# Packed attention and a GELU feed-forward on one core: pair 0's output tiles stored by four transfers of 32 rows each, its values loaded in two transfers, and a new order of all engines

## The chip, the cores and the metric

The kernel runs on one core of one Trainium2 chip. The metric is the device time of one launch in microseconds (us); a time given for a kernel is the median of several runs. A core has five engines with a program each: TensorE (PE, with its weight loads PEld), VectorE (DVE), ScalarE (ACT), GpSimd (POOL) and SyncE (SP). In this kernel all transfers are issued from SP's queue, and sixteen DMA engines move the bytes.

## What is computed

```python
def sm_attn(qq, kk, vv):
    s = scale * np.matmul(qq, kk.transpose(0, 1, 3, 2))
    s = s - np.max(s, axis=-1, keepdims=True)
    a = np.exp(s)
    a = a / (np.sum(a, axis=-1, keepdims=True) + 1e-09)
    return np.matmul(a, vv)
p_packed = sm_attn(p, k, v)            # 32 packed queries over 576 keys
out = sm_attn(q, p_packed, p_packed)   # 576 queries over the 32 packed rows

x = out.transpose(0, 2, 1, 3).reshape(4608, 512)
h = x @ w_in                           # w_in 512 x 2048
g = 0.5 * h * (1.0 + erf(h / sqrt(2)))
return g @ w_out                       # w_out 2048 x 512
```

q, k and v are 8 batches x 8 heads x 576 x 64, p is 8 x 8 x 32 x 64, all fp32. The output is 4608 x 512.

## The kernel before

The eight batches are worked off in four pairs (`pr` 0 to 3). A pair has 1152 tokens, which make nine output tiles of 128 x 512, kept in the accumulators `acc_<pr>_<i>`. d_ff is worked off in four units of 512 columns in each pair, so there are 16 units of 8 steps, 32 steps a pair. A unit makes h from the attention weights `a2T` and from `wp` (the packed rows times w_in, made from `wps`), h in six or twelve products of 128 x 288 (L1080); ACT and DVE make g of it; and the products with w_out (`o`, L1133 to L1135, three for each tile since fp32 values are split in a high and a low part) go to PSUM and are added to the accumulators by DVE (L1197). Tile 4 of a pair, the edge tile, gets half its rows from each batch; it is made last in a unit (`o_edge`).

The attention of the next pair is worked in between the products of the present one: p is loaded (L501) and transposed on PE (`pTm`, L507), k and q are loaded (L424 for pair 0, one transfer each; L434 for the later pairs, four transfers of 32 partitions each) and transposed (on PE in pair 0, by DVE later), v is loaded (`load_values`). The weights of a unit come as raw words in pair 0 (`wraw`, L939 and L943), are decoded into a high and a low part, and stored to scratch memory (`ws<-w`, L995); from pair 1 on they are reloaded from there (`w<-ws`, L917).

For pair 0, rows are held in another order than in memory: a tile has four blocks of 32 rows, each of which goes to every 18th row of the output. `finish.store` (L1204 to L1209) writes such a tile in one transfer of 4 x 32 x 512, and tile 4, whose blocks lie in two batches, in two of 2 x 32 x 512. The later pairs write 128 x 512 in one transfer (L1204). The values of pair 0 are loaded by `sixths` (L484): 96 partitions, four heads, 384 numbers in a row (1536 bytes).

The order of the instructions on each engine is set at build time by a planner, `Order`. Every piece of work is an `Op` with an engine, a model cost and a due step; the tables `FIRST` (pair 0), `SECOND` (pair 1) and `LATER` (pairs 2 and 3) hold the due steps of the attention's parts, and `LEAD`, `PATIENCE`, `STEADY`, `DMA_SLACK` and `DMA_EARLY` are rules for all of them. The planner keeps the model that eight DMAs at most are under way (`DMA_DEPTH`): in the program, each transfer on SP is issued when the one eight places ahead of it has landed. Where the model finds PE without work before the first g is used, `keep_warm` puts in products on constants (`idle<-still`, L1053), which I call fillers; in the start, other products are also made twice, once into a tile named `idle`.

Of the kernel before, what the change touches and what calls it, by code (L numbers as in the profile page):

```python
# [19 lines left out]
P = 128  # L20
B, H, S, D = 8, 8, 576, 64
PK = 32
# [3 lines left out]
NB32 = S // 32  # L26
# [13 lines left out]
PE, ACT, DVE, POOL, DMA = "PE", "ACT", "DVE", "POOL", "DMA"  # L40
# [2 lines left out]
DMA_FIRST, DMA_ISSUE, DMA_START, DMA_END, DMA_RATE = 2.0, 0.5, 0.6, 0.9, 390e3  # L43

DMA_DEPTH = 8
DMA_SLACK, DMA_EARLY = 4.0, 60.0
TABLE_SWITCH = 1.3
PE_START, PE_WINDOW, PE_LEAST = 1.0, 3.41, {True: 0.45, False: 0.9}
IDLE, IDLE_END = 0.11, 150.0
# [2 lines left out]


LATER = {
    "p": (-39.26, -15.86),
    "k": (5.65, 1.31, 12.01, 17.16),
    "v": (-16.69, 1.61, 22.03, 27.81),
    "q": (22.44, 3.57, 12.78, 22.93),
    "scores1": (14.09, -17.44),
    "softmax1": (-9.54, 26.63, -24.19, 26.51),  # L60
    "packed": (-23.89, -22.94, 27.45, 26.53),
    "scores2": (-14.65, 21.78),
    "softmax2": (-24.19, -0.03, 50.16, 22.74),
    "weights2": (29.03, 29.95, 1.17, -15.25),
    "groups1": ((0,), (1,), (2,), (3,)),
    "groups2": ((0, 1), (2, 3)),
}

SECOND = {
    "p": (-3.61, -10.72),  # L70
    "k": (3.41, 0.25, 20.0, -56.69),
    "v": (-22.26, 3.59, 18.15, 21.3),
    "q": (23.11, 21.3, 21.6, 7.77),
    "scores1": (-9.82, -56.39),
    "softmax1": (-18.51, 6.58, 9.15, -41.24),
    "packed": (-34.85, 15.81, -9.92, 9.75),
    "scores2": (9.45, 41.41),
    "softmax2": (-24.65, -40.94, -56.99, -10.3),
    "weights2": (22.04, 35.39, 45.19, 24.77),
    "groups1": ((0, 1), (2, 3)),  # L80
    "groups2": ((0, 1), (2, 3)),
}

AHEAD = 12
LEAD = {"load": 18.5, "decode": -13.4, "packed_w_in": 60.1}

PATIENCE = {PE: -23.4, ACT: -9.6, DVE: 24.2, POOL: 77.7, DMA: 2.3}
STEADY = {PE: 45.5, ACT: -6.9, DVE: -15.7, POOL: 21.7, DMA: -10.7}

FIRST = {  # L90
    "p": (-210.0, -176.51),
    "k": (-233.78, -212.77, -176.19, -173.89),
    "v": (-186.03, -193.47, -169.61, -153.18),
    "q": (-191.58, -185.11, -162.68, -170.97),
    "w": (-199.98, -187.11, -191.97, -183.54, -185.21, -163.81, -39.7, -122.51),
    "scores1": (-152.97, -209.53, -175.46, -197.7),
    "softmax1": (-160.37, -231.56, -191.55, -215.45),
    "packed": (-171.95, -190.55, -210.03, -179.55),
    "scores2": (-212.47, -194.44, -189.26, -176.97),
    "softmax2": (-173.59, -208.41, -192.11, -160.67),  # L100
    "weights2": (-189.27, -209.73, -175.76, -227.21),
    "decode": (-202.23, -169.16, -49.02, -171.27, -8.54, -68.27, -164.29, -169.26),
    "packed_w_in": (-177.55, -176.04, -176.11, -179.23),
    "weights_split": (-184.5, -170.67, -166.39, -169.56),
    "groups1": ((0,), (1,), (2,), (3,)),
    "groups2": ((0,), (1,), (2,), (3,)),
    "gpsimd": (0, 1),
    "copy": ("DVE", "DVE", "DVE", "ACT"),
    "banks": (False, False, True, False),
    "turn": {"k": ("ACT", "DVE", "ACT", "ACT"), "q": ("ACT", "DVE", "ACT", "ACT")},  # L110
}

# [51 lines left out]
class Order:  # L164
# [4 lines left out]
    def __init__(self):  # L169
# [4 lines left out]
        self.warm, self.window, self.busy, self.idle = False, PE_WINDOW, 0.0, None  # L174
        self.port, self.tiled, self.patience = 0.0, False, PATIENCE
        self.free[PE] = PE_START
# [5 lines left out]
    def start(self, task, then=None):  # L182
        self.open += 1
        self.advance(task, then, None, None)

    def fire(self, event):
        event.count -= 1
        if event.count == 0:
            for fn in event.waiting:
                self.at(self.now, fn)  # L190
# [121 lines left out]
def packed_attention_gelu_ffn(ctx: ExitStack, tc: tile.TileContext, q, k, v, p, w_in, w_out, out):  # L312
# [12 lines left out]
    nc = tc.nc  # L325
# [142 lines left out]
    def values_of(t):  # L468

        main = t[:, 0:16 * D].rearrange("p (g t d) -> p g t d", g=4, t=4)  # L470
        tail = t[:64, 16 * D:20 * D].rearrange("p (g d) -> p g d", g=4)
        return main, tail

    def sixths_of(t):

        if len(t.shape) > 2:
            t = t.rearrange("p a b c -> p (a b c)").bitcast(F32)
        return t[:96, 0:24 * D].rearrange("p (g t d) -> p g t d", g=4, t=6)

    def load_values(s, step):  # L480
        heads = slice(4 * s.hh, 4 * s.hh + 4)

        def sixths(t):
            nc.sync.dma_start(  # L484
                sixths_of(t).rearrange("p g t d -> p g (t d)"), v[s.b, heads].rearrange("g (p t) d -> p g (t d)", t=6))

        def fn(t):
            main, tail = values_of(t)
            nc.sync.dma_start(
                main.rearrange("p g t d -> p g (t d)"), v[s.b, heads, 0:512].rearrange("g (p t) d -> p g (t d)", t=4))  # L490
            nc.sync.dma_start(tail, v[s.b, heads, 512:S].rearrange("g p d -> p g d"))

        cost, fn = ((1, 640e3), sixths) if s.b < 2 else ((2, 900e3, 0.6), fn)
        s.v = yield Op(DMA, cost, step, fn, [(s.v_ring, f"v_{s.n}")])
        fire(s.v_loaded)

# [317 lines left out]
    def held(task, step):  # L814
        if step >= 1:
            yield reached[min(int(step), NU * 8 - 1)]
        yield from task

    def attention(pr, plan):
# [11 lines left out]
        for s in ss:  # L831
            s.mx, s.mx2 = mx, mx2
            s.v_ring = wps[1] if (s.b, s.hh) == (0, 1) else vraws
            start(held(load_values(s, plan["v"][s.i]), plan["v"][s.i]))
# [64 lines left out]
    def parts_of(i):  # L899

        return 2 if i < 2 else 1
# [6 lines left out]
    def weight(u, i, load_steps, steps):  # L908


        ring_, home, k = (wis, wi, i) if i < 2 else (wos, wo, i - 2)
        n, f = f"{u}_{i}", u % NF
        if u >= NF:
            yield stored[f, i]
            home[u, k] = yield Op(
                DMA, (1, 524e3), steps[0],
                lambda t: nc.sync.dma_start(t.bitcast(F32), scratch[f, i]), [(ring_, f"w_{n}")])  # L917
            for part in range(parts_of(i)):
                fire(w_ready[u, i, part])
            return  # L920
        yield [decode(u, i, part, *at) for part, at in enumerate(zip(load_steps, steps))]
        d = scratch[f, i] = dram.tile([P, 2, FB], F32, name=f"ws_{f}_{i}")
        start(keep(f, i, d, home[u, k], steps[-1] + 4))
# [213 lines left out]
    def output_steps():  # L1137
        for n in range(NU * 8):
# [3 lines left out]
            if n == STEPS + NC4:  # L1142
                order.patience = STEADY
            if n % STEPS == 0:
# [44 lines left out]
    def finish(u, i, t, ring_, n):  # L1189
        pr, f = divmod(u, NF)  # L1190
        x = t[:, 0] if ring_ is wide else t
        if f == 0:
            acc[pr, i] = yield Op(ACT, 0.48, n, lambda a: nc.scalar.copy(a, x), [(accs, f"acc_{pr}_{i}")])
            ring_.give(t)
            return
        a = acc[pr, i]
        yield Op(DVE, 0.6, n, lambda: nc.vector.tensor_tensor(a, x, a, ALU.add))  # L1197
        ring_.give(t)
        if f == NF - 1:
            r0 = pr * 2 * S + i * P  # L1200

            def store():
                if pr > 0:
                    nc.sync.dma_start(out[r0:r0 + P], a)  # L1204
                    return
                for r, m in ((0, P),) if i != 4 else ((0, 64), (64, 64)):
                    b, n0 = divmod((r0 + r) // PK, NB32)
                    rows = out[b * S:(b + 1) * S].rearrange("(x n) d -> n x d", n=NB32)[n0:n0 + m // PK]
                    nc.sync.dma_start(rows, a[r:r + m])  # L1209

            yield Op(DMA, (1, 262e3), n, store)
            accs.give(a)


# [16 lines left out]
    for u in range(NU):  # L1231
        for i in range(6):
            use = 8 * u + (2 * i - 6 if i < 2 else i - 3)
            if u == 0:
                part = slice(2 * i, 2 * i + 2) if i < 2 else slice(2 + i, 3 + i)
                start(weight(u, i, FIRST["w"][part], FIRST["decode"][part]))
            else:
                start(held(weight(
                    u, i, *([use + k - LEAD[name] for k in range(parts_of(i))] for name in ("load", "decode"))),
                    8 * u - AHEAD))  # L1240
# [6 lines left out]
        else:  # L1247
            for j in range(2):
                start(held(packed_w_in(u, j, 0, 8 * u + 4 * j - LEAD["packed_w_in"]), 8 * u + 4 * j - AHEAD))
    start(hidden_steps())  # L1250
# [34 lines left out]
```

## Time and profile before

| | |
|---|---|
| median of 3 runs | 750.29 us (749.0, 750.29, 750.57) |
| the profiled execution's own time | 751.05 us |
| its span, from the first to the last instruction | 749.3 us |
| mean granted clock of PE | 0.991 of full speed |
| transfers | 106.77 MB, 142 GB/s over the span |

The profile comes from one execution. PE, DVE, ACT, POOL and SP are the engines named above; L12 is a line of the kernel. A row of a timeline or of the chain has the start in us, the length in us, and what ran; in brackets is the idle time ahead of it and what ended it. "SPq" is time in which SP's queue issues transfers. A row of a table of stretches has the stretch, its length, busy us and number of instructions of PE, PEld, DVE, ACT and POOL, then the granted clock of PE, the busy share of the sixteen DMA engines and GB/s. In a table of one tile, three numbers between slashes are the shortest, the median and the longest duration in ns, and then stand the first and last start in us. Rows of transfers end with how long it took from issue to landing.

### The profile page before, as it was taken

The numbers are of one execution on the slowest core, as the hardware profiler recorded it, in microseconds if no ns is written. First come the engines' busy times: TensorE is split into PE (matmuls) and PEld (weight loads), VectorE is DVE, ScalarE is ACT, GpSimd is POOL, SyncE is SP. The second block draws the span as 40 slices with busy tenths as digits, with TensorE's granted clock in tenths as the row PEclk, the third lists the DMA queues.
The fourth block names the chain that finished last, engine by engine and source line by source line (L and its number), as shares of the span: only waits on it lengthen the run. The fifth ranks groups of instructions, "written<-read, shape, count | busy, mean of one in ns | idle before, by whom it ended". The sixth has DMA issues, their size and how long they took to land.

```text
span 749.3 us, 13343 instructions
## 1 busy us (share of the span) xinstructions
PE 730.7 (98%) x5369; PEld 592.8 (79%) x5369; DVE 399.1 (53%) x608; ACT 363.2 (48%) x606; POOL 153.0 (20%) x330
## 2 busy tenths in 40 slices
PE   8899999999999699999999999999999999999998
PEld 6667788787877578887877888877877888888886
DVE  3689958777778231435484622454474821333332
ACT  4577785657654433355453543364543543333221
POOL 1353545455410101101100111100011110111010
PEclk9899999999999999999999999999999999999999
DMA  9977966489924577189223986179233603122022
GB/s 272 329 264 137 238 144 225 169 232 243 210 101 150 147 111 173 31 188 140 77 96 115 239 116 165 34 178 165 45 113 117 238 3 101 68 71 72 1 91 92
DMA packets 154449, 106.77 MB, mean 142 GB/s; under 512 B 122644, under 2 KB 130324, under 8 KB 154388
## 3 DMA queue, kind: packets, MB, share of 16 engines
q1 hardware_dynamic: 154388, 105.93, 55.0%
q8 instruction: 42, 0.69, 0.4%
q14 instruction: 19, 0.16, 0.1%
HBM read 83.89 MB, written 22.02 MB: 141 GB/s over the span
## 4 chain that ended last, share of the span: by engine, by line
PE 92%; DMA 4%; SPq 3%; DVE 1%; ACT 1%; issue 0%; ACTq 0%
PE h L1080 25%; PE o L1133 17%; PE o L1135 15%; PE o L1134 15%; PE wps L1014 4%; DMA p<-in_p_dram 2%; PE s L535 2%; SPq L434 2%; PE o_edge L1133 2%; PE o_edge L1135 2%; PE o_edge L1134 2%; DMA v<-in_v_dram 2%; PE idle L1053 2%; PE pp L677 1%; PE e1Tm L636 1%; PE h L1071 1%
## 5 line engine op out<-in xcount | busy, mean ns | idle before, releaser
L1080 PEld LDWEIGHTS h<-a2T,wp 128*128 128x128 f32 x1488 | 209.8, 188 | 9.6
L1080 PE MATMUL h<-a2T,wp 128*128 128x288 f32 x1488 | 216.5, 295 | 0.0
L1103 ACT ACTIVATE graw<-h 128x576 f32<-128x576 f32 x127 | 82.8, 652 | 273.4 <-PE h L1080 216.7
L1133 PE MATMUL o<-w,g 128*128 128x512 f32 x508 | 207.2, 408 | 0.0
L1135 PE MATMUL o<-w,g 128*128 128x512 f32 x508 | 199.7, 393 | 0.0
L1134 PE MATMUL o<-w,g 128*128 128x512 f32 x508 | 199.4, 393 | 0.0
L1112 DVE TENSOR_TENSOR g<-graw,g 128x512 fp32r<-128x512 f32 x128 | 90.4, 706 | 200.2 <-ACT g L1110 193.6
L1123 POOL CAST t<-graw 128x64 fp32r<-128x64 f32 x128 | 36.2, 282 | 493.9 <-ACT graw L1103 399.6
L1133 PEld LDWEIGHTS o<-w,g 128*128 128x128 f32 x508 | 95.7, 188 | 42.4 <-issue 24.7
L1135 PEld LDWEIGHTS o<-w,g 128*128 128x128 f32 x508 | 95.6, 188 | 22.6 <-DVE g L1112 0.9
L1134 PEld LDWEIGHTS o<-w,g 128*128 128x128 f32 x508 | 95.9, 189 | 15.0
L1197 DVE TENSOR_TENSOR acc<-o,acc 128x512 f32<-128x512 f32 x96 | 63.9, 686 | 40.2 <-PE o L1135 39.9
L1110 ACT CAST g<-graw 128x512 fp32r<-128x512 f32 x128 | 79.4, 621 | 3.8 <-PE o L1135 0.9
L1030 DVE TENSOR_TENSOR wp<-wps,wp 128x1024 fp32r<-128x1024 f32 (+1 forms) x32 | 37.8, 1187 | 20.9 <-ACT wp L1025 20.8
L1124 POOL TENSOR_TENSOR t<-graw,t 128x64 fp32r<-128x64 f32 x128 | 45.6, 356 | 10.2
L1025 ACT CAST wp<-wps 128x1024 fp32r<-128x1024 f32 (+1 forms) x31 | 30.8, 1000 | 16.6 <-PE wps L1014 16.6
L1014 PE MATMUL wps<-w,pp 64*32 64x512 f32 (+1 forms) x544 | 34.9, 576 | 0.0
L976 POOL TENSOR_TENSOR w<-wt 128x512 int32<-128x512 int32 x16 | 22.5, 1404 | 42.3 <-DVE wt L962 38.4
L1053 PE MATMUL idle<-still 128*128 128x256 bf16 x205 | 29.3, 293 | 1.1 <-DVE still L394 1.1
L949 ACT ACTIVATE wt<-wraw 128x512 f32<-128x512 f32 x32 | 21.7, 679 | 15.3 <-DMA wraw<-in_moe_w_in_dram 9.1
L957 DVE TENSOR_SCALAR wt<-wt 128x512 int32<-128x512 int32 x32 | 28.3, 883 | 1.1
L984 POOL TENSOR_TENSOR wt<-wt 128x512 int32<-128x512 int32 x16 | 21.8, 1361 | 28.5 <-DVE wt L962 25.6
(126 smaller groups left out, 673.1 us busy)
## 6 DMA issues: line engine op xcount, KB each, us to landing
w<-ws SPq DMA_DIRECT2D x72, 512.0 KB, 5.2
ws<-w SPq DMA_DIRECT2D x24, 512.0 KB, 5.9
out_dram<-acc SPq DMA_DIRECT2D x35, 256.0 KB, 2.1
wraw<-in_moe_w_in_dram SPq DMA_DIRECT2D x16, 512.0 KB, 9.1
wraw<-in_moe_w_out_dram SPq DMA_DIRECT2D x16, 512.0 KB, 4.2
k<-in_k_dram SPq DMA_DIRECT2D x48, 144.0 KB, 5.8
q<-in_q_dram SPq DMA_DIRECT2D x48, 144.0 KB, 4.6
v<-in_v_dram SPq DMA_DIRECT2D x12, 512.0 KB, 4.7
```

The costliest lines, as they stand in the source:

```text
L1014: nc.tensor.matmul(t[r0:r0 + 32, hh, :m], lhsT=pp[b][rows, hh, r0:r0 + 32], rhs=wi[u, hh][rows, g, cols], start=True, stop=True)
L1030: yield Op(DVE, 0.16 + 1.04 * m / FB, step, lambda: nc.vector.tensor_tensor(lo, x, hi.bitcast(F32), ALU.subtract))
L1053: nc.tensor.matmul(bank(t)[:, :256], lhsT=still[:, :P], rhs=still, start=True, stop=True)
L1080: nc.tensor.matmul(t[:, half, :HALF], lhsT=w[:, wpart, ch, fc], rhs=a2T[b, ch][:, apart, half * HALF:(half + 1) * HALF], start=ch == 0 and ...
L1103: lambda raw: nc.scalar.activation(raw.rearrange("p (a n) -> p a n", a=2), t[:, :, :HALF], AF.Gelu),
L1110: g = yield Op(ACT, 0.52, lead, lambda g: nc.scalar.copy(g[:, 0], main), [(gts, f"g_{n}")])
L1112: DVE, 0.6, lead, lambda: nc.vector.tensor_tensor(g[:, 1], main, g[:, 0].bitcast(F32), ALU.subtract),
L1124: nc.gpsimd.tensor_tensor(dst[:, 1], side, dst[:, 0].bitcast(F32), ALU.subtract)
L1133: nc.tensor.matmul(t, lhsT=g[0], rhs=w[:, 0], start=first, stop=False)
L1134: nc.tensor.matmul(t, lhsT=g[0], rhs=w[:, 1], start=False, stop=False)
L1135: nc.tensor.matmul(t, lhsT=g[1], rhs=w[:, 0], start=False, stop=last)
L1197: yield Op(DVE, 0.6, n, lambda: nc.vector.tensor_tensor(a, x, a, ALU.add))
```

## The change

The nine output tiles of pair 0 are each stored by four transfers of one 32-row block, so that ten transfers become 36, and their cost in the planner's model is changed with it. The values of pair 0 are loaded in two transfers, the first four and the last two of each six rows (runs of 1024 and of 512 bytes). All due steps of the three tables and the rules `LEAD`, `PATIENCE` and `STEADY` have other numbers, `DMA_SLACK` and `DMA_EARLY` are smaller, and in pair 0 other engines make some copies. Lines from L484 on stand three lines lower in the new kernel.

```diff
-DMA_SLACK, DMA_EARLY = 4.0, 60.0
+DMA_SLACK, DMA_EARLY = 2.0, 50.0
...
-LEAD = {"load": 18.5, "decode": -13.4, "packed_w_in": 60.1}
+LEAD = {"load": 41.5, "decode": -5.8, "packed_w_in": 12.3}
...
-    "v": (-186.03, -193.47, -169.61, -153.18),
+    "v": (-249.99, -74.38, -178.71, -155.31),
...
-    "gpsimd": (0, 1),
-    "copy": ("DVE", "DVE", "DVE", "ACT"),
-    "banks": (False, False, True, False),
+    "gpsimd": (0,),
+    "copy": ("ACT", "DVE", "DVE", "DVE"),
+    "banks": (False, True, True, True),
...
         def sixths(t):
-            nc.sync.dma_start(
-                sixths_of(t).rearrange("p g t d -> p g (t d)"), v[s.b, heads].rearrange("g (p t) d -> p g (t d)", t=6))
+            src = v[s.b, heads].rearrange("g (p t) d -> p g t d", t=6)
+            for part in (slice(0, 4), slice(4, 6)):
+                nc.sync.dma_start(
+                    sixths_of(t)[:, :, part].rearrange("p g t d -> p g (t d)"),
+                    src[:, :, part].rearrange("p g t d -> p g (t d)"))
...
-        cost, fn = ((1, 640e3), sixths) if s.b < 2 else ((2, 900e3, 0.6), fn)
+        cost, fn = ((2, 700e3), sixths) if s.b < 2 else ((2, 900e3, 0.6), fn)
...
-                for r, m in ((0, P),) if i != 4 else ((0, 64), (64, 64)):
+                for r in range(0, P, PK):
                     b, n0 = divmod((r0 + r) // PK, NB32)
-                    rows = out[b * S:(b + 1) * S].rearrange("(x n) d -> n x d", n=NB32)[n0:n0 + m // PK]
-                    nc.sync.dma_start(rows, a[r:r + m])
-
-            yield Op(DMA, (1, 262e3), n, store)
+                    rows = out[b * S:(b + 1) * S].rearrange("(x n) d -> n x d", n=NB32)[n0]
+                    nc.sync.dma_start(rows, a[r:r + PK])
+
+            yield Op(DMA, (1, 262e3) if pr else (4, 262e3), n, store)
```

SP's queue at the end of pair 0, before the change: `acc` are the output tiles, `w` and `ws` the reloaded weights, `k` and `p` those of the batches that come next; "x4" is four transfers.

```order
L917 DMA w_4_2887<-ws_4_845 128x1024
L1209 DMA out_dram<-acc_8_1414 4x32x512
L917 DMA w_5_2896<-ws_5_834 128x1024
L917 DMA w_2_2902<-ws_2_1260 128x1024
L917 DMA w_3_2905<-ws_3_1340 128x1024
L1209 DMA out_dram<-acc_4_1454 2x32x512 x2
L434 DMA k_1_2941<-in_k_dram 32x36x32 x4
L501 DMA p_2979<-in_p_dram 128x2x64 x2
```

The same place in the new order:

```order
L434 DMA k_0_2912<-in_k_dram 32x36x32 x4
L1212 DMA out_dram<-acc_7_1348 32x512 x4
L1212 DMA out_dram<-acc_8_1375 32x512 x4
L1212 DMA out_dram<-acc_4_1418 32x512 x4
L920 DMA w_4_3028<-ws_4_923 128x1024
L920 DMA w_5_3040<-ws_5_938 128x1024
L920 DMA w_2_3052<-ws_2_1297 128x1024
L920 DMA w_3_3054<-ws_3_1347 128x1024
L504 DMA p_3167<-in_p_dram 128x2x64 x2
```

The k load has moved ahead of the stores and the four reloads of w behind all of them, so that p, the last row, follows the reloads of w instead of k.

PE around the transpose of that p (`pTm`), before:

```order
L1135 MATMUL o_3_2922<-w_5_2896,g_3008 128x512
L1080 MATMUL h_3074<-a2T_0_2996,wp_1_2760 128x288 x6
L1080 MATMUL h_3074<-a2T_1_2947,wp_1_2760 128x288 x6
L507 MATMUL pTm_3093<-ident,p_2979 128x128 x2
L1133 MATMUL o_0_3098<-w_2_2516,g_3061 128x512
```

PE there in the new order:

```order
L1138 MATMUL o_2_3203<-w_2_2367,g_3093 128x512
L1136 MATMUL o_3_3208<-w_2_2367,g_3093 128x512
L1137 MATMUL o_3_3208<-w_2_2367,g_3093 128x512
L1138 MATMUL o_3_3208<-w_2_2367,g_3093 128x512
L510 MATMUL pTm_3212<-ident,p_3167 128x128 x2
L1136 MATMUL o_0_3176<-w_3_2371,g_3127 128x512
```

Counted from unit 3's edge tile, 18.8 us of PE's work stood ahead of the transpose; now it is 20 groups of three `o` products, six sets of twelve `h` and two of `wps`.

SP's queue in the start, before (`v_1` are the values of batch 0's heads 4 to 7, `p_151` is the second batch's p):

```order
L424 DMA k_0_85<-in_k_dram 128x1152
L424 DMA k_1_87<-in_k_dram 128x1152
L501 DMA p_91<-in_p_dram 128x2x64 x2
L943 DMA wraw_0_0_98<-in_moe_w_in_dram 128x2x512
L484 DMA v_1_102<-in_v_dram 96x4x384
L943 DMA wraw_1_0_107<-in_moe_w_in_dram 128x2x512
L424 DMA q_0_111<-in_q_dram 128x1152
L943 DMA wraw_0_1_115<-in_moe_w_in_dram 128x2x512
L484 DMA v_0_121<-in_v_dram 96x4x384
L939 DMA wraw_2_0_136<-in_moe_w_out_dram 128x1024
L943 DMA wraw_1_1_139<-in_moe_w_in_dram 128x2x512
L501 DMA p_151<-in_p_dram 128x2x64 x2
```

The new order from the second batch's p on (`p_144`; ahead of it stand the same kinds of loads with one v, `v_0`, in two pieces):

```order
L504 DMA p_144<-in_p_dram 128x2x64 x2
L424 DMA q_1_171<-in_q_dram 128x1152
L424 DMA k_0_198<-in_k_dram 128x1152
L942 DMA wraw_2_0_218<-in_moe_w_out_dram 128x1024
L942 DMA wraw_3_0_236<-in_moe_w_out_dram 128x1024
L424 DMA k_1_257<-in_k_dram 128x1152
L486 DMA v_1_275<-in_v_dram 96x4x256
L486 DMA v_1_275<-in_v_dram 96x4x128
```

`v_1` has moved from the fifth row of SP's order to its eighteenth and nineteenth. On PE, the fillers of the start are 231 where they were 205, and the required products are the same.

More of the change, by code (lines that the diff above doesn't have):

```diff
@@ L54 @@
 LATER = {
[L55 to L65, printed above, removed]
+    "p": (11.96, 4.31),
+    "k": (9.37, 6.72, -0.79, 5.76),
+    "v": (4.46, 5.97, 10.35, 23.09),
+    "q": (7.94, 14.96, 23.74, 28.45),
+    "scores1": (-2.56, 15.38),
+    "softmax1": (8.43, -1.96, 4.16, 5.99),
+    "packed": (-50.68, -7.0, 15.26, 19.97),
+    "scores2": (22.79, 15.93),
+    "softmax2": (-77.33, -62.89, 23.22, 15.85),
+    "weights2": (32.15, -50.98, -6.98, 38.51),
+    "groups1": ((0, 1, 2, 3),),
     "groups2": ((0, 1), (2, 3)),
@@ L69 @@
 SECOND = {
[L70 to L81, printed above, removed]
+    "p": (20.75, 3.34),
+    "k": (7.37, -42.06, 10.92, 22.21),
@@ L82 @@
+    "v": (8.64, 9.54, 12.08, 14.62),
+    "q": (24.0, -36.23, 19.77, 24.5),
+    "scores1": (-7.96, 8.69),
+    "softmax1": (23.58, 28.48, 10.35, 11.22),
+    "packed": (13.43, 9.46, -19.64, 17.8),
+    "scores2": (-42.32, 23.44),
+    "softmax2": (3.08, -54.42, 7.07, 36.08),
+    "weights2": (7.31, 23.91, -34.4, 27.85),
+    "groups1": ((0,), (1,), (2,), (3,)),
+    "groups2": ((0,), (1,), (2,), (3,)),
 }
 AHEAD = 12
-LEAD = {"load": 18.5, "decode": -13.4, "packed_w_in": 60.1}
-PATIENCE = {PE: -23.4, ACT: -9.6, DVE: 24.2, POOL: 77.7, DMA: 2.3}
@@ L88 @@
-STEADY = {PE: 45.5, ACT: -6.9, DVE: -15.7, POOL: 21.7, DMA: -10.7}
+LEAD = {"load": 41.5, "decode": -5.8, "packed_w_in": 12.3}
+PATIENCE = {PE: -50.7, ACT: -58.2, DVE: 28.6, POOL: 30.2, DMA: -16.5}
+STEADY = {PE: 50.0, ACT: -44.9, DVE: 8.1, POOL: -12.5, DMA: 13.9}
 FIRST = {
-    "p": (-210.0, -176.51),
-    "k": (-233.78, -212.77, -176.19, -173.89),
-    "v": (-186.03, -193.47, -169.61, -153.18),
[L94 to L105, printed above, removed]
+    "p": (-317.54, -182.89),
+    "k": (-327.51, -303.62, -196.02, -185.2),
+    "v": (-249.99, -74.38, -178.71, -155.31),
+    "q": (-216.51, -212.03, -93.83, -161.52),
+    "w": (-194.95, -219.42, -192.91, -163.65, -152.43, -145.84, -71.43, -169.98),
+    "scores1": (-221.37, -193.05, -72.18, -73.16),
+    "softmax1": (-51.37, 6.81, -347.66, -175.1),
+    "packed": (-180.43, -262.75, -182.09, 5.22),
+    "scores2": (-233.03, -212.25, -155.17, -251.0),
+    "softmax2": (-146.14, -327.21, -189.22, -190.15),
+    "weights2": (-183.99, -138.74, -180.16, -74.68),
+    "decode": (-178.03, -74.98, -180.05, -168.82, -193.1, -214.82, -193.35, 17.95),
+    "packed_w_in": (-192.13, -218.39, -190.45, -146.14),
+    "weights_split": (-94.13, -184.63, -65.79, -335.34),
+    "groups1": ((0, 1), (2, 3)),
```

## The prediction

> **What bounds the kernel now.** I read the page's busy shares, slices and chain of work first, then the waits of PE, then the chain around the longest wait.
>
> ```profile
> PE 730.7 (98%) x5369; PEld 592.8 (79%) x5369; DVE 399.1 (53%) x608; ACT 363.2 (48%) x606; POOL 153.0 (20%) x330
> PE   8899999999999699999999999999999999999998
> PEclk9899999999999999999999999999999999999999
> PE 92%; DMA 4%; SPq 3%; DVE 1%; ACT 1%; issue 0%; ACTq 0%
> ```
>
> PE is busy 98% of a span of 749.3 us and is 92% of the chain; no other engine is above 53%. So the time is PE's own work plus the little time in which it waits or runs at a lower clock. Only two places show in the slices: the first two or three, and slice 14 with its "6". The waits of PE over the whole run name them (what waited for what, us in total, times, the longest):
>
> ```profile
> PE pTm L507 <- DMA p<-in_p_dram: 10.6, 3, 6.6
> PE e1Tm L636 <- ACT graw L1103: 1.4, 2, 0.7
> PE idle L677 <- DMA v<-in_v_dram: 0.9, 1, 0.9
> ```
>
> The timeline of PE shows where the two long waits for p end, and a table of stretches shows the clock around them (busy us per engine with counts, then granted clock, DMA share, GB/s):
>
> ```profile
> 24.01 0.66 PE L507 MATMUL pTm<-ident,p 128*128 128x128 f32 x2 [3.38 <-DMA p<-in_p_dram]
> 262.79 0.66 PE L507 MATMUL pTm<-ident,p 128*128 128x128 f32 x2 [6.60 <-DMA p<-in_p_dram]
> ```
>
> ```profile
> 23.20:30.00 6.80, 5.99 (x28) 5.30 (x29) 2.61 (x6) 4.83 (x10) 1.35 (x2) 0.50 1.01 404
> 258.70:265.50 6.80, 2.71 (x8) 2.26 (x9) 2.40 (x3) 0.00 (x0) 0.00 (x0) 0.50 1.29 163
> 62.00:237.00 175.00, 175.00 (x1274) 140.50 (x1273) 138.34 (x198) 110.89 (x188) 72.45 (x103) 1.00 0.73 184
> 0.00:62.00 62.00, 55.02 (x687) 41.61 (x688) 39.44 (x78) 36.83 (x77) 24.15 (x31) 0.94 0.91 279
> ```
>
> Each wait has a half-clock stretch with it. The second costs 6.60 us of idleness and, of the 2.71 us that PE then ran at 0.50, half: 1.35 us. From 62 to 237 us PE waits for nothing at full clock. The first 62 us are a start in which the transfers are the limit (DMA share 0.91).
>
> Why the second wait exists is read from the chain around it, "SPq" being time in which SP's queue issues transfers:
>
> ```profile
> 237.44 0.58 DVE acc L1197
> 242.33 2.28 SPq L1209
> 244.65 3.96 SPq L434
> 248.66 6.53 SPq L434
> 255.23 2.95 SPq L434
> 258.97 0.57 SPq L501
> 259.58 3.07 DMA p<-in_p_dram
> ```
>
> After pair 0's last addition (237.44) SP issues the stores of its last output tiles (L1209), then a k load in four pieces (L434), then p (L501). Those four pieces take from 244.65 to 258.86, while a timeline of SP shows the same form elsewhere at a third of it:
>
> ```profile
> 94.87 4.17 SPq L434 DMA_DIRECT2D q<-in_q_dram  x4
> 244.65 14.21 SPq L434 DMA_DIRECT2D k<-in_k_dram  x4
> ```
>
> A transfer is issued only when the one eight places before it has landed, and eight before these pieces are the stores and reloads of w. The stretches say why those land late:
>
> ```profile
> 213.50:222.00 8.50, 8.50 (x96) 7.09 (x81) 6.50 (x12) 5.88 (x9) 0.56 (x2) 1.00 0.26 99
> 253.00:255.00 2.00, 2.00 (x13) 1.72 (x12) 0.69 (x1) 2.00 (x5) 0.29 (x1) 1.00 0.14 53
> 397.00:399.00 2.00, 2.00 (x15) 1.77 (x13) 0.43 (x1) 0.00 (x0) 0.00 (x0) 1.00 0.90 348
> ```
>
> While pair 0's 4x32x512 stores run, 0.26 of the sixteen DMA engines are busy (four), during the 2x32x512 halves 0.14 (two); pair 1's 128x512 stores of the same bytes have 0.90. So **the pair-0 store is a narrow transfer that plugs an eight-deep queue**, and p stands behind it.
>
> A rule of the Trainium skill ("DMA: Bandwidth & Descriptors", "Rules for kernel authors") says the same of the shape: the outermost dimension sets how many DMA engines a transfer uses. Its 4 and 2 agree with the 0.26 and 0.14 here. The same table speaks against the change: it advises coalescing small transfers and calls two transfers to disjoint partitions useless. By that advice alone four stores of 64 KB would gain nothing; by the rows above the old one never had the sixteen engines, so I don't follow it.
>
> **The change part by part.** *Stores.* A 32x512 piece has 32 rows outermost, so I expect it to spread as the 128x512 one does. SP's cost per store:
>
> ```profile
> L1204 SPq DMA_DIRECT2D out_dram<-acc x27: 332/337/874, 392.2 to 746.4; - x27
> L1209 SPq DMA_DIRECT2D out_dram<-acc x10: 537/568/2279, 210.1 to 242.3; - x10
> DMA to landing us min/median/max: 2.0/2.1/5.8
> ```
>
> Ten issues become 36. At 0.34 to 0.57 us each, the twelve behind the last output tiles (acc_7, acc_8, acc_4) take 4.1 to 6.8 us of SP, against four pieces of k that took 14.21 and are now issued ahead of them. They land in about 2 us, so the queue moves. The order also puts p later on PE. Between unit 3's edge tile (237.42) and its p, PE before had 18.8 us of work (to 256.19, where the wait begins), while p arrived 25.4 us after the edge. In the new order this work is 20 groups of three o products, six sets of twelve h and two wps:
>
> ```profile
> 200.15 1.60 PE h L1080 x12
> 202.45 1.02 PE wps L1014 x16
> 203.47 0.43 PE o L1133
> 204.36 0.24 PE o L1133
> ```
>
> o is 0.23 (0.43 right after wps, a switch of 0.20), so 60 x 0.23 + 6 x 1.59 + 2 x 1.22 = 25.8 us. Behind the edge, p has DVE's addition (0.6), four stores (1.4 to 2.3), four reloads of w and its own issue and landing ahead of it. Reloads have these rows:
>
> ```profile
> w<-ws SPq DMA_DIRECT2D x72, 512.0 KB, 5.2
> DMA to landing us min/median/max: 3.0/5.3/11.3
> ```
>
> With the reloads landing at the median this is 0.6 + 2.3 + 4 x 0.57 + 5.3 + 3.1 = 13.6 us, at the worst landing 19.6; both are under 25.8. So the wait of 6.60 and the 1.35 behind it go: **-7.95 us**. The next one to be late would be w_4: it is used 8 groups of o, four sets of h and one wps after the edge, 5.5 + 6.4 + 1.2 = 13.1 us, and lands after 0.6 + 1.4..2.3 + 0.3 + 3.0..11.3 = 5.3..14.5 us. At the median it has 4 us to spare, at the end of the range it costs 1.4.
>
> *Fillers and switches.* PE's required products are the same in both orders. The order has 231 warm-up products (L1053) where it had 205, and 57 changes from a narrow product to a wide one where it had 67.
>
> ```profile
> L1053 PE MATMUL idle<-still 128*128 128x256 bf16 x205 | 29.3, 293 | 1.1 <-DVE still L394 1.1
> 36.24 1.36 PE L1053 MATMUL idle<-still 128*128 128x256 bf16 x11
> ```
>
> Products overlap, so a filler's price is its pitch. The 11 of the second row take 1.36 us with the tail of the last one, which the next piece overlaps (its mean of 0.293 less the 0.143 that each adds to busy time: 0.15), so 1.21 us or 0.11 each; 0.143 (29.3 over 205) is the upper bound, and nothing the lower, where PE would have waited for a load anyway. 26 x 0.11 = **+2.9 us** (0 to +3.7). Ten switches at 0.20: **-2.0 us** (-2.0 to 0, as they may stand where PE waits). Which engines make the copies of the start (copy, banks, gpsimd) changes too; the only waits of PE on them in the list are 1.4 us in all for L636, so I take 0.
>
> *Values in two transfers, and the start.* The chain of the first 24 us is two rows:
>
> ```profile
> 3.39 8.31 DMA v<-in_v_dram
> 11.71 12.16 DMA p<-in_p_dram
> ```
>
> ```profile
> 30.88 0.88 PE L677 MATMUL pp<-v,e1T 96*32 96x64 f32 x48
> ```
>
> Everything queued ahead of that second p shares one full pipe, so its landing is set by the bytes. The new order has one v (0.59 MB, about 2 us at 279 GB/s) less ahead of it. PE reaches it sooner by about as much, 1 to 2 us by my estimate: products of v and e1T like these (0.88 a set), some transposes and two fillers have gone behind it. So I take the 3.38 us and its 5.99/2 = 3.0 us of half clock as unchanged: **0**. v now has runs of 1024 and 512 B instead of 1536. No row shows such a pair; the nearest is the later pairs' own two v transfers, whose issues are among the ordinary ones, and a shorter run costs issue (0.33 us) at least. The v of batch 0's heads 4 to 7, fifth row of SP's order before, is now its eighteenth and nineteenth: issued at about 21 to 22.5 us, where before's rows of that place stand,, landing 5 to 12.2 us later (the rows of w and p), so at 26 to 35 us. Before, PE's products on it stand at 30.88; the new order has 2 to 5 us more of fillers and other products ahead of them, so PE wants it at about 33 to 36 (an estimate). I take 0; bounds for the whole start are -3.0 (the half clock goes) and +5 (v 2 us late, and a half clock of 3.0 as after 24 us).
>
> *Margins.* DMA_SLACK and DMA_EARLY let the planner issue loads later; its loads now stand about 2 us nearer their use. Before, PE waited for none of them outside the places above, and 62 to 237 us is full without a gap, so the cover is there; if it is gone in places (k for DVE, w_4, v behind sixteen stores), a few waits of 1 to 3 us come. I take 0, bounds 0 and +6. The end of the kernel (stores of 128x512) is the same.
>
> The sum against the profiled run: -7.95 + 2.9 - 2.0 + 0 + 0 = -7.05 us. Its span of 749.3 becomes 742.25 and its own time of 751.05 becomes 744.0. The three timed runs have a median of 750.29, 0.76 below that profiled run, so the forecast is **743.2 us**.
>
> **The rivals.** *The start keeps its clock.* If p lands slightly sooner (one v less ahead of it), its wait of 3.38 us may no longer cost the half-clock stretch: -3.0, so about 740. For it: the two stretches, of 6.8 us each, stand with waits of 3.38 and 6.60, and no wait of 0.9 or less has one. Against it: PE gets there sooner too. The Trainium skill ("TensorE: Matmul & The Clock Gate", "Part 1: The HAM clock gate") puts the bound at one idle window of about 3.4 us in a free-running count; the 3.38 here lies on it, so the row leaves it open.
>
> *Partly given back.* w_4 and the k loads behind twelve stores, each landing at its worst, cost 1.4 to 6 us: 745 to 749.
>
> *It does not do what it says.* If a 32-row store uses few DMA engines too, 16 stores in place of 4 plug the queue the same way, and the p wait stays: +2.9 - 2.0 = 0.9 above the median, or up to 2 less where the longer cover of PE helps, 749 to 751. Against it: the 128x512 rows with 0.90.
>
> *Slower: the start waits for values.* The place is PE's first product on the v that moved back.
>
> ```profile
> 23.39 5.03 SPq L995 DMA_DIRECT2D ws<-w  x2
> ```
>
> If SP is held there as it was in the two issues of w's first stores (5.03 us), v is issued near 30 instead of 22 and with the 12.16 us of p's landing arrives at 42 or later, where PE wants it by 34.5. In this start the wait counts one to one, for every product of the first unit hangs on it, and a second half clock costs 3.0. The price is -7.05 + 3.0 + (landing - 34.5): it turns slower than before from a landing at 38.6, and landings of 41 to 45 give 752 to 757. For it: those two durations, both from this stretch. Against it: in the new order v stands ahead of that store, and only two loads of w and two of k are queued right before it.
>
> **How the numbers follow.** Forecast (741 to 746) 0.55; the start keeps its clock (738.5 to 741) 0.13; partly given back (746 to 748.8) 0.12; does not do it (749 to 751) 0.09; slower start (752 to 757) 0.11. The range 738.5 to 750 holds all but the slower start and a part of the case before it, about 0.83. About 0.2%, 1.5 us, is what a measurement of this kernel can tell from no change: faster 0.8, same 0.09, slower 0.11.
>
> **What would show it.** Right: no wait of PE near 256 us, the granted clock 1.00 there, DMA share during pair 0's stores near 0.9, SP's L434 issues back near 4 us for four, and the first wait for p still 2.5 to 3.4 us. Wrong: a share of 0.26 or less during the stores; a wait of PE for w, k or v between 240 and 262; a second v row of several us among the waits at 33 to 40 us; or a wait for p at another pair's boundary.

## The result and the profile after

| kernel | median | runs | ratio to before (95% interval) |
|---|---|---|---|
| before | 750.43 us | 749.0 to 752.48 (4) | 1 |
| changed | 739.11 us | 737.92 to 740.66 (4) | 0.9848 (0.9819 to 0.9878) |
| changed, a second time, before at 749.43 us | 738.07 us | 736.56 to 738.53 (5) | 0.9855 (0.9834 to 0.9876) |

The kernel became 1.5% faster, 11.3 us by the medians. The forecast of 743.2 us had the direction and the place, the range held the time, and the gain was 11.3 where 7.1 was forecast. The profiled execution took 740.66 us, the longest of its four runs, with a span of 738.9 us; against the profiled execution before that is 10.4 us.

The page of the changed kernel, with its busy shares, slices and chain:

```profile
PE 728.0 (99%) x5395; PEld 592.4 (80%) x5395; DVE 399.6 (54%) x604; ACT 357.4 (48%) x600; POOL 149.5 (20%) x328
PE   7999999999999999999999999999999999999998
PEclk8999999999999999999999999999999999999999
PE 95%; DMA 3%; SPq 1%; issue 1%; DVE 0%; ACT 0%
```

The "6" in slice 14 is gone. The waits of PE over the whole run:

```profile
PE km L461 <- DMA k<-in_k_dram: 3.1, 1, 3.1
PE idle L461 <- DMA k<-in_k_dram: 1.2, 1, 1.2
PE idle L1056 <- DVE still L394: 1.1, 1, 1.1
PE idle L680 <- issue: 1.0, 1, 1.0
PE h L1083 <- ACT graw L1106: 0.8, 1, 0.8
```

No wait for p is left, neither at the boundary nor in the start. A wait that was not there before, 3.1 us for a k load, stands in the start. Its place on PE's timeline, and the clock behind it (a table of stretches, as before):

```profile
9.39 2.15 PE L461 MATMUL km<-ident,k 128*128 128x128 f32 x9 [3.08 <-DMA k<-in_k_dram]
```

```profile
8.60:15.40 6.80, 6.00 (x49) 3.25 (x49) 3.29 (x6) 1.23 (x2) 0.00 (x0) 0.50 1.08 310
211.00:213.00 2.00, 2.00 (x42) 0.81 (x30) 1.90 (x4) 1.01 (x1) 0.00 (x0) 1.00 0.51 124
239.00:241.00 2.00, 2.00 (x15) 1.88 (x14) 1.97 (x4) 0.73 (x2) 0.00 (x0) 1.00 0.59 135
```

So a half-clock stretch of 6.8 us is still in the start of this execution, some 15 us sooner than before. The last two rows lie inside pair 0's stores: 0.51 and 0.59 of the DMA engines are busy where it was 0.26 and 0.14. SP's timeline at the end of pair 0:

```profile
205.68 9.86 SPq L1212 DMA_DIRECT2D out_dram<-acc  x16
232.94 3.97 SPq L434 DMA_DIRECT2D k<-in_k_dram  x4
237.01 5.83 SPq L1212 DMA_DIRECT2D out_dram<-acc  x12
242.94 1.83 SPq L920 DMA_DIRECT2D w<-ws  x4
244.82 1.09 SPq L504 DMA_DIRECT2D p<-in_p_dram  x2
```

The four pieces of k take 3.97 us instead of 14.21, and p is issued at 244.82 instead of 258.97.

Three parts went into the change: the stores, the split of the values, and the order. For each experiment below that edits the store or the values alone, the other engines execute the same sequence as in the kernel it starts from; SP's differs by the transfers named.

### The profile page after: what moved, and what is told of

The parts are those of the page before. It is cut to its first block, busy times and chain, and to the rows that moved or that the text cites. A ratio compares the mean times of both kernels' runs of the same rounds, so it can differ in the third digit from the quotient of the medians.

```text
span 738.9 us, 13425 instructions
## 1 busy us (share of the span) xinstructions
PE 728.0 (99%) x5395; PEld 592.4 (80%) x5395; DVE 399.6 (54%) x604; ACT 357.4 (48%) x600; POOL 149.5 (20%) x328
## 4 chain that ended last, share of the span: by engine, by line
PE 95%; DMA 3%; SPq 1%; issue 1%; DVE 0%; ACT 0%
PE h L1083 26%; PE o L1136 17%; PE o L1138 16%; PE o L1137 16%; PE wps L1017 4%; PE s L538 2%; PE o_edge L1136 2%; PE o_edge L1138 2%; PE o_edge L1137 2%; PE idle L1056 2%; DMA k<-in_k_dram 2%; DMA wraw<-in_moe_w_out_dram 2%; PE pp L680 2%; PE e1Tm L639 1%; PE h L1074 1%
## 5 line engine op out<-in xcount | busy, mean ns | idle before, releaser
L1083 PEld LDWEIGHTS h<-a2T,wp 128*128 128x128 f32 x1488 | 209.6, 188 | 11.4 <-ACT graw L1106 1.0
L1115 DVE TENSOR_TENSOR g<-graw,g 128x512 fp32r<-128x512 f32 x128 | 93.7, 734 | 212.4 <-ACT g L1113 212.2
L1028 ACT CAST wp<-wps 128x1024 fp32r<-128x1024 f32 x30 | 30.1, 1014 | 22.4 <-PE wps L1017 22.4
L1056 PE MATMUL idle<-still 128*128 128x256 bf16 x231 | 31.8, 288 | 1.1 <-DVE still L394 1.1
L1056 PEld LDWEIGHTS <-still 128*128 128x128 bf16 x231 | 22.8, 102 | 9.1 <-issue 4.5
L960 DVE TENSOR_SCALAR wt<-wt 128x512 int32<-128x512 int32 x32 | 25.4, 792 | 1.1
```

The lines of the kernel that those rows point to most:

```text
L1056: nc.tensor.matmul(bank(t)[:, :256], lhsT=still[:, :P], rhs=still, start=True, stop=True)
L1083: nc.tensor.matmul(t[:, half, :HALF], lhsT=w[:, wpart, ch, fc], rhs=a2T[b, ch][:, apart, half * HALF:(half + 1) * HALF], start=ch == 0 and ...
L1115: DVE, 0.6, lead, lambda: nc.vector.tensor_tensor(g[:, 1], main, g[:, 0].bitcast(F32), ALU.subtract),
```

## The experiments

**The new stores alone, in the old order.** `finish.store` of the changed kernel put into the kernel before:

```diff
-                for r, m in ((0, P),) if i != 4 else ((0, 64), (64, 64)):
+                for r in range(0, P, PK):
                     b, n0 = divmod((r0 + r) // PK, NB32)
-                    rows = out[b * S:(b + 1) * S].rearrange("(x n) d -> n x d", n=NB32)[n0:n0 + m // PK]
-                    nc.sync.dma_start(rows, a[r:r + m])
+                    rows = out[b * S:(b + 1) * S].rearrange("(x n) d -> n x d", n=NB32)[n0]
+                    nc.sync.dma_start(rows, a[r:r + PK])
```

> The kernel before with one edit: pair 0's tiles are stored by four transfers of 32 rows; the order of all engines stays as before. Theory (the old store used few DMA engines and plugged the queue): the 6.60 us wait of PE for p at the boundary goes, since k's four pieces take 4 us again and p lands about 12 us after the edge tile where PE gets to it after 18.8; with the 1.35 us of half clock that is -8 us, 742 to 743, and the DMA share during the stores is near 0.9. Rival (transfers that wait for the one eight places ahead: four times as many of them plug it as before): the wait stays, 749 to 752, at a share of about 0.26.

Measured: 740.8 us beside 749.95 (ratio 0.9871, 0.9853 to 0.9890). The theory holds: the stores alone bring most of the gain, 9.2 us where 8 were expected. One part of it fails: the DMA share during the new stores is 0.58 from 212 to 214 us, and not near 0.9. SP's timeline of this kernel shows k's pieces at 6.16 us and p issued nine microseconds sooner than before, and in the stretch from 236 to 266 us PE is busy throughout at full clock:

```profile
243.37 6.16 SPq L434 DMA_DIRECT2D k<-in_k_dram  x4
249.62 1.15 SPq L501 DMA_DIRECT2D p<-in_p_dram  x2
```

```profile
236.00:266.00 30.00, 30.00 (x186) 24.58 (x185) 14.56 (x22) 14.82 (x23) 3.35 (x12) 1.00 0.91 185
```

**As many transfers, but narrow.** Is it the width or the number of transfers? The same place, cut by columns:

```diff
-                    nc.sync.dma_start(rows, a[r:r + m])
+                    part = 128 if m == P else 256
+                    for c in range(0, 512, part):
+                        nc.sync.dma_start(rows[:, :, c:c + part], a[r:r + m, c:c + part])
```

> The kernel before with one edit: pair 0's tiles are stored by four transfers each, cut by columns (4x32x128, tile 4 in 2x32x256), so as many transfers and bytes as with 32 rows each, but with 4 and 2 outermost as in the old store. Theory (the width counts): the DMA share stays near 0.26 and 0.14, the wait for p at the boundary stays 6 us or grows, 750 to 756. Rival (smaller transfers free the queue's places sooner): the wait goes, 742 to 744.

Measured: 750.06 us beside 749.95 (1.0008, 0.9996 to 1.0020). Nothing is gained. Of the stretches of this kernel, the first lies inside its stores, the second at the boundary:

```profile
215.00:217.00 2.00, 2.00 (x15) 1.89 (x14) 0.66 (x2) 1.99 (x3) 0.00 (x0) 1.00 0.28 85
236.00:266.00 30.00, 22.88 (x126) 18.77 (x125) 12.72 (x19) 11.06 (x17) 2.23 (x8) 0.89 0.78 182
```

The share of 0.28 is again little more than four engines of sixteen, and in its list of waits p has one of 7.1 us. The width counts; four times the transfers without it change nothing. Their runs are shorter too, 512 bytes instead of 2048, and that was not tried apart from the width.

**The old store in the new order.** The first edit undone in the changed kernel.

> The changed kernel with one edit: pair 0's tiles are stored by one transfer each (tile 4 by two) as before; the new order of all engines stays. Theory: the narrow stores plug the queue again, w_4 is late behind them and PE waits 1 to 5 us between 240 and 262, 740 to 744. Rival 1 (the order alone, with p later on PE and k ahead, would have hidden them): within 0.7 us of the changed kernel. Rival 2 (only the store counts): all 8 us come back, 747.

Measured: 746.49 us beside 749.95 (0.9967, 0.9948 to 0.9987); the new order and the split values without the stores are worth 0.3%. The waits of PE that the changed kernel doesn't have, on this one's timeline:

```profile
223.36 0.90 PE L680 MATMUL pp<-v,e1T 128*32 128x64 f32 x40 [2.36 <-DMA v<-in_v_dram]
258.15 0.50 PE L1136 MATMUL o<-w,g 128*128 128x512 f32 x1 [3.92 <-DMA w<-ws]
```

The 3.92 us for w are what the theory named (1 to 5 us). They are not all: a v load is 2.36 us late as well, and each of the two waits is followed by 3.41 us at half clock, with PE busy, so 1.7 us more each. That is 9.7 us in this execution. It took 749.72 us and is one of four at 749.7 to 750.2; the other eight lie at 744.2 to 747.4. So it shows where the 7.4 us between the two medians (of two groups) can come from, and not what an average run has of each. The time is nearer to rival 2's 747, but p is not what waits.

**The split of the values alone, in the old order.**

```diff
-            nc.sync.dma_start(
-                sixths_of(t).rearrange("p g t d -> p g (t d)"), v[s.b, heads].rearrange("g (p t) d -> p g (t d)", t=6))
+            src = v[s.b, heads].rearrange("g (p t) d -> p g t d", t=6)
+            for part in (slice(0, 4), slice(4, 6)):
+                nc.sync.dma_start(
+                    sixths_of(t)[:, :, part].rearrange("p g t d -> p g (t d)"),
+                    src[:, :, part].rearrange("p g t d -> p g (t d)"))
```

> The kernel before with one edit: the values of pair 0 are loaded in two transfers of shorter runs; the order stays. Theory: within 0.7 us of before, since the start is limited by bytes and these are the same. Rival (shorter runs and four more transfers in an eight-deep queue slow the start): PE's waits in the first 62 us grow and it is 1 to 4 us slower.

Measured: 747.27 us beside 749.95 (0.9966, 0.9951 to 0.9982): faster, which neither expected. On its timeline the second p of the start comes 1.6 us sooner than before (24.01):

```profile
22.38 0.66 PE L510 MATMUL pTm<-ident,p 128*128 128x128 f32 x2 [2.88 <-DMA p<-in_p_dram]
259.68 0.66 PE L510 MATMUL pTm<-ident,p 128*128 128x128 f32 x2 [5.60 <-DMA p<-in_p_dram]
```

The second row is the wait at the boundary. It is 1.0 us shorter than before (6.60), so 1.0 of the 2.7 us may be the boundary's, by one execution each; beside the new stores, which remove that wait, it can't count.

**Both edits of code in the old order.**

> The kernel before with both edits of code and the old order: pair 0's tiles stored by 32 rows, its values loaded in two transfers. Theory (the two gains of 9.2 and 2.7 us add, and the new order adds nothing of its own): 738 us, ratio 0.984, as fast as the changed kernel. Rival (the new order is worth the 3 us that the two changes of code don't explain): 740 to 742, ratio 0.987 to 0.989.

Measured: 738.92 us beside 748.24 (0.9876, 0.9853 to 0.9898). The theory by its time, the rival by its ratio: before was 1.7 us faster in this group than in the last. Undecided, so it was run again, together with the stores alone and the changed kernel.

> The changed kernel itself, once more, as the reference of this group: 738 to 740 us, ratio 0.985 as measured first; PE's first long wait is again for the second k (2 to 3 us near 9 us) with or without a half-clock stretch behind it.

> Once more the old order with both edits of code, now beside the changed kernel. The new order was forecast to cost 0.9 us by fillers and switches where no wait goes: by the forecast's terms this kernel is 0.9 us faster than the changed one. Theory (the order alone is worth nothing that can be measured): within 1 us of it either way. Rival (the new order brings the 2 to 3 us that the forecast missed): 2 to 3 us slower than the changed kernel.

> Once more the old order with the new stores alone, beside the same with the split values too. Theory (the split lets the second p of the start land 1.6 us sooner, and so saves the wait and at times a half-clock stretch): 1 to 3 us slower than that kernel. Rival (the 2.7 us of the split alone came from the luck of the start): within 0.7 us of it.

| one group, before at 749.43 us | median | ratio (95% interval) |
|---|---|---|
| changed | 738.07 us | 0.9855 (0.9834 to 0.9876) |
| old order, stores and values | 739.03 us | 0.9869 (0.9848 to 0.9890) |
| old order, stores alone | 740.2 us | 0.9890 (0.9871 to 0.9908) |

The steps are 9.2 us for the stores, 1.2 for the values and 1.0 for the order; the intervals of neighbours overlap, so the last two are small and not proven by the times. For the values the traces say more. In the old order PE's second p began in four profiled executions with one v transfer at 24.01, 23.04, 23.46 and 22.82 us, in three with two at 22.38, 22.19 and 21.96: by the means 1.2 us sooner, without overlap. The row of the last group with the stores alone, and that with both edits:

```profile
23.46 0.66 PE L507 MATMUL pTm<-ident,p 128*128 128x128 f32 x2 [3.35 <-DMA p<-in_p_dram]
```

```profile
21.96 0.58 PE L510 MATMUL pTm<-ident,p 128*128 128x128 f32 x2 [2.30 <-DMA p<-in_p_dram]
```

Why it lands sooner was not tried. In the trace the two weight loads queued ahead of p are issued 2 to 3 us later, since two more transfers take places among the eight; that fewer bytes then compete with p is argued only.

**One v transfer in the new order.** The split undone in the changed kernel.

> The changed kernel with one edit: the values of pair 0 are loaded in one transfer as before; the new order stays. Theory (what the split gave the old order was that its second p landed 1.6 us sooner, and in the new order PE doesn't wait for that p): within 1 us of the changed kernel, 738 to 740. Rival (the split is worth 2.7 us in any order): 741.5 to 742.5.

Measured: 739.21 us beside 748.24 (0.9869, 0.9849 to 0.9889). The time lies in the theory's 738 to 740; but the ratio overlaps that of the changed kernel, 0.9848 and 0.9855, and also what a loss of 2.7 us would give (0.988), so it is inconclusive.

**Fillers of half the size.** The changed kernel with

```diff
-                nc.tensor.matmul(bank(t)[:, :256], lhsT=still[:, :P], rhs=still, start=True, stop=True)
+                nc.tensor.matmul(bank(t)[:, :128], lhsT=still[:, :P], rhs=still[:, :128], start=True, stop=True)
```

> The changed kernel with one edit: each of the 231 fillers has 128 columns in place of 256; the order stays. Forecast's price (a filler costs its pitch of 0.11 us on the path): half of it is saved for most, 6 to 12 us, 727 to 733. Rival 1 (the start is bound by its transfers, a filler costs nothing there): PE waits as much longer, within 1.5 us of the changed kernel. Rival 2 (the gaps that open cost the clock): a second stretch at 0.50 in the first 62 us, 1 to 4 us slower.

Measured: 736.23 us beside 748.24 (0.9837, 0.9818 to 0.9857), 3.0 us under the kernel above in the same group; by the ratios it is 0.8 to 1.4 us under the changed kernel. The forecast's price fails: by their pitch 231 x 0.055 = 12.7 us should have gone, and at most a quarter did; rival 1 is nearest. Against the changed kernel's second profiled execution, by PE's starts, the fillers take 11.8 us less, but the waits 5.3 more and the other products 3.8 more (1.7 of it a half-clock stretch). These are the two largest of ten waits in the start:

```profile
4.83 0.87 PE L461 MATMUL idle<-ident,k 128*128 128x128 f32 x3 [1.89 <-DMA k<-in_k_dram]
20.52 0.66 PE L510 MATMUL idle<-ident,p 128*128 128x128 f32 x2 [2.47 <-DMA p<-in_p_dram]
```

**Fillers where PE waited.** The changed kernel with 24 fillers ahead of the transposes of the late k, written into the same tile:

```diff
         def product(m):
+            if name == "km_0_1_0":
+                for _ in range(24):
+                    nc.tensor.matmul(m[:, :256], lhsT=still[:, :P], rhs=still, start=True, stop=True)
             for n in range(3):
```

> The changed kernel with one edit: 24 more fillers (about 2.6 us) ahead of the transposes of batch 0's second k, where PE waited 3.08 us and then ran 6 us at half clock. Theory (the clock falls because PE stands still for over 3 us): the wait shrinks to about 0.5 us, no stretch at 0.50 follows, and the profiled run is 3 us shorter; the median 1 to 3 us lower, 736 to 738, with all runs at a mean clock of 0.998 or more. Rival (the half clock comes from elsewhere, as from the start of the program): the same time within 0.7 us, and the stretch at 0.50 stays.

Measured: 738.16 us beside 748.24 (0.9858, 0.9838 to 0.9878). The wait is gone, no stretch at 0.50 follows, and all five runs have a mean clock of 0.999 or 1.000. But p now waits, at 20.55:

```profile
20.55 0.41 PE L513 MATMUL idle<-ident,p 128*128 128x128 f32 x2 [1.35 <-DMA p<-in_p_dram]
```

The profiled run is 3.9 us shorter than the changed kernel's first one, but the median lies just above the theory's 736 to 738: in time it can't be told from the changed kernel, four of whose five runs in the last group kept the clock without it.

**Both, and the fillers small only after the first 90.** The last edit, and in `keep_warm`:

```diff
+                fillers.append(1)
+                m = 256 if len(fillers) <= 90 else 128
...
```

> The changed kernel with 24 more fillers ahead of the second k's transposes and with the fillers after the first 90 at 128 columns. Theory (late in the start nothing but the fillers holds PE: the 140 or so that come later give 0.055 us each, less some 2 us of waits for loads and DVE that then show, and the clock keeps at 1.00): 3 to 6 us faster than the changed kernel, 733 to 736. Rival (other engines set the start's end, waits take it all): within 1 us of the kernel with 24 more fillers.

Measured: 735.32 us (734.39 to 737.31) beside 749.43, 0.9825 (0.9802 to 0.9847): 2.75 us under the changed kernel of its group, just short of the theory's 3 to 6. It has the lowest median of all kernels here, though its interval still overlaps that of the changed kernel. With the clock at 1.00, PE's busy time from 40 to 62 us falls to

```profile
40.00:62.00 22.00, 19.60 (x298) 15.00 (x297) 20.62 (x35) 16.96 (x31) 9.73 (x12) 1.00 0.92 216
```

19.6 us, while DVE has 20.62, so that there PE is no longer the busiest engine. Whether DVE is the next limit was not tried.

## Why the prediction was right, and where its sizes were off

*The wait of 6.60 us and its 1.35 us of half clock: right.* The chain was read correctly: narrow store, plugged queue, late k pieces, late p. The stores alone remove it, narrow ones in the same number don't. One step inside was wrong: the share during the new stores isn't near 0.9 but 0.51 to 0.59. The 16 pieces of the first four tiles took SP 9.86 us, 0.62 apiece with the waits for a place, where I had 0.34 to 0.57. The twelve at the end took 5.83 us, 0.49 apiece; 64 KB in 0.49 us are 135 GB/s, which is the rate of the row from 239 to 241 us. So it is the issue, by these numbers, that keeps the share down. It was enough.

*w_4 next: right.* With the old store in the new order the long wait behind the edge is for w, 3.92 us, and with the new store there is none for w. The twelve stores at the end took 5.83 us, within 4.1 to 6.8. But the working put the edge tile's four stores alone ahead of w_4, and in the queue all twelve stand there: the w loads are issued from 242.94 on, some 6 us behind the edge tile's last product, and not 2 to 3. The spare time was enough all the same.

```profile
236.64 0.39 PE L1138 MATMUL o_edge<-w,t 128*128 128x512 f32 x1
```

*Fillers +2.9, switches -2.0: near, and by luck.* Changed kernel against old order with both edits, in the last group: by PE's starts in the traces, fillers take 2.0 us more, the other products 3.7 less, waits 0.5 more. Of the 3.7, 1.7 are a half-clock stretch of the old order's profiled execution, which leaves the -2.0; that these are the switches was not tried. The pitch of 0.11 us was right, and its use as a price was not: half-size fillers gave back at most a quarter of what it promised, so a filler on the path costs 0.03 us or less. Much of what they take, PE would have waited anyway: 5.3 of the 11.8 us came back as waits. The order was forecast at +0.9 and measured at -1.0, both too small to tell from nothing.

*The values, 0: the step that failed.* The working weighed the shorter runs and the bytes, and not what two more transfers do to the others of an eight-deep queue. In the old order they let the second p come 1.2 us sooner, which is 1.2 us by the medians in the last group and 2.7 alone, of which 1.0 may be the boundary's. In the new order, the one that was forecast, the experiment with one v transfer leaves their worth open.

*The start's wait for p, "unchanged": wrong in the mechanism.* That wait is gone in the profiled execution (1.7 us in the second one), because k_1, now queued behind the first p, is what PE meets first and waits for; where fillers stand in that wait, PE waits 1.35 us for p. That the term came out near 0 in the profiled execution is luck: 3.08 us for k and 6.00 us of work at half clock stand where 3.38 and 5.99 stood for p. The values at rows eighteen and nineteen, the place of the slower rival, caused no wait for v in the changed kernel's two profiled executions; at products on v the lists have 1.0 and 0.7 us of "issue" and name no load.

*From the profiled run to the median: 0.76 us was too little on one side.* The profiled executions of both kernels have a half-clock stretch in the start, but not every run has one. In the last group, the seven runs of before at a mean clock of 0.990 to 0.992 have a median of 749.68 us, the four at 0.994 or 0.995 have 747.26. The changed kernel's profiled execution (0.995) was its slowest run, 1.55 us above the median. Of the changed kernel's nine runs five have a mean clock of 0.999 or 1.000, where the start kept it, three have 0.997 and one 0.995. So the time fell into the band of the rival in which the start keeps its clock (738.5 to 741), and in most runs it did so in whole or in part. What it hangs on in the two traces is the wait for k (3.08 us with the half clock, 1.62 without), and not a p that lands sooner. The rival's price of 3.0 us is about what separates these two executions (740.66 and 737.81).

By parts then, where -7.1 was forecast: stores -9.2, values -1.2, order -1.0, which is -11.4 in the last group. Of the stores' 9.2, 7.95 are the boundary as the profile before shows it; the rest is within what the start changes from run to run.

## What to carry to other kernels

When an engine waits for a small load, look at what is queued ahead of it and how many DMA engines that uses: the store at fault was off the critical path, landed without any engine waiting for it, and cost 8 us through the places that it held. Read the price of idle-time fillers from a run that shrinks them, never from their pitch. And where a stretch at half clock comes and goes, compare medians of several runs with the clock beside them, since one profile is one throw.

## What the hardware showed beyond this

The half clock keeps to a count, and the length of a wait alone doesn't say what follows it. In the start, waits of 3.15 and 3.16 us had 3.41 us of half clock behind them, and one of 2.88 us had 6.83. In all fourteen profiled executions the stretches at half clock last 3.41 or 6.83 us, and each begins a whole number of steps of 3.41 us after the moment at which the clock is first granted in full. What decides, by these traces, is how long PE stands still within one such step. There are fourteen steps at full clock with 1.99 us or more of idleness before the kernel's end, and each was followed by half clock; none of the others was, up to 1.81 us. A step at half clock with 0.67 us of idleness or less ended the stretch, and one with 0.80 or more let it go on.

Four rows show the bound, from the new order with the old store. PE's idle time is the length of the row less its busy time: 1.81 us in the first, after which the clock stays, and 1.99 in the third, after which it is halved:

```profile
6.33:9.74 3.41, 1.60 (x14) 1.31 (x12) 0.66 (x2) 0.86 (x2) 0.00 (x0) 1.00 1.13 249
9.74:13.15 3.41, 3.41 (x52) 1.96 (x50) 1.86 (x5) 0.87 (x2) 0.00 (x0) 1.00 1.04 370
221.37:224.78 3.41, 1.42 (x43) 1.17 (x44) 2.14 (x3) 1.58 (x5) 0.79 (x5) 1.00 0.19 67
224.78:228.19 3.41, 3.41 (x17) 2.17 (x23) 1.11 (x2) 1.26 (x3) 0.00 (x0) 0.50 0.00 0
```

In the second run of the old order with the new stores alone, a wait of 3.35 us lies across the end of a step, 2.02 us ahead of it and 1.33 behind, and costs two steps:

```profile
18.72:22.13 3.41, 1.39 (x53) 0.94 (x50) 1.41 (x4) 1.53 (x5) 1.26 (x1) 1.00 1.07 367
22.13:25.54 3.41, 2.08 (x10) 1.87 (x11) 1.31 (x4) 1.52 (x4) 0.00 (x0) 0.50 1.03 410
25.54:28.96 3.42, 3.42 (x18) 2.91 (x17) 0.89 (x2) 3.31 (x7) 1.34 (x2) 0.50 1.02 411
```

So waits of about the same length cost one step at half clock or two, depending on where they fall in the count. By these bounds even a wait of 3.6 us would cost none if it lay evenly across the end of a step; that is an estimate from the 1.81 us, and no execution here shows it. The count may also be why the start's clock changes between runs of one kernel, which most runs, without a trace, can't show.

By the Trainium skill ("TensorE: Matmul & The Clock Gate", "Part 1: The HAM clock gate") the clock halves after at least one idle window of about 3.4 us. The step of 3.41 us agrees with it; the idleness doesn't, since about 2 us of it within a step were enough. Here the measurement decides.
